# A third attention slot in four steps of the first block: attention one unit further ahead of the MoE loop

## The chip, the core and the metric

One core of a Trainium2 chip runs the whole program. The metric is the device time of one execution in microseconds (us). Of the engines, TensorE (PE; its weight loads are listed as PEld), VectorE (DVE), ScalarE (ACT), GpSimd (POOL) and the queues that issue DMAs (SP, POOL, ACT) appear below.

## What is computed

The reference chains three layers over 2304 tokens (4 batches of 576) with 512 features, in float32:

```python
scores = scale * q @ k.T                      # 8 heads of 64 columns
scores = where(0 <= pos_q - pos_k < 64, scores, -1e9)
attn = exp(scores - max); attn = attn / (sum(attn) + 1e-9)
x = attn @ v                                  # to (2304, 512)
h = x @ w_in                                  # (512, 2048)
g = where(h >= 1, h, where(h <= -1, 0, (h + 1)**2 / 4))
x = g @ w_out                                 # (2048, 512)
h = x @ w_in2                                 # (512, 1024)
solu = h * softmax(h)
out = (layernorm(solu) * g_ln) @ w_out2       # (1024, 512)
```

The window of 64 positions makes attention cheap: a tile of 192 queries needs 256 keys.

## The kernel before

**Tiling.** Tokens are cut into 12 tiles of 192 (`TT`), and two tiles make one of 6 blocks of 384 (`NB`, `NBLK`). Attention works in *units* g = 0 to 47: one tile and one pair of heads, four units to a tile, eight to a block. From unit 18 on (`PU` = 9) two units are done as one *pair*, P = g/2. The first MoE layer runs per block j over 16 slices f of the hidden size.

**One unit** has these stages, and each needs the one before it: S(g) (`st_s`), scores on PE into a PSUM bank, then three masked reductions with a running maximum on DVE (L360), then three exponentials on ACT (L366); norm (`st_norm`), a sum, a reciprocal and a product on DVE (L377, L378, L386); T(g) (`st_t`), three transposes on PE (L402) and a copy on ACT (L407); V(g) (`st_v`), the product with v on PE (L421), then the high part xh of x on ACT (L428) and the low part xl on DVE (L429). `st_qkt` transposes q and k for a later unit on DVE (L317, L326) into one of two buffers `kq0` and `kq1`. For a pair the scores are pS (`pair_s`: L442 on PE, L452 on DVE, L458 on ACT) and the product is pV (`pair_v`, L476).

**One MoE step** (j, f) is H(j,f), 12 matmuls into one bank (`moe_h`, L496: every float32 product is done as high·high + high·low + low·high), the activation on ACT and DVE (L505, L506, L511, L512), the low part of g (L516, on POOL in block 0, on DVE later), and two steps afterwards Y(j,f), 12 matmuls into four accumulators (`moe_y`, L527). After f = 15 the accumulators are copied out (`moe_out`, L537 and L539) and stored. In block 0 the weights of this layer arrive from DRAM as 64-bit numbers and are converted on ACT (L132, L145) and DVE (L136, L137, L146: the lower parts), one unit of weights for `w_in` and one for `w_out` per slice.

**Order.** The code is a list of steps `seq`: block 0 first in two half blocks for f = 0 and 1, then in whole steps f = 2 to 15, then blocks 1 to 5. The generator `slots` cuts the attention into slots, four of them per unit up to unit 16; a step takes `n0` slots before its weight conversion and `n1` after it, one each, and block 0 takes exactly 40, which ends with T(16) and S(17). A scheduler then orders each engine's instructions: it takes the first in the code's order whose inputs and buffers it expects to be ready. Every engine executes its list in that order.

**PSUM.** Block 0 has two banks for attention (`ps_at`), two for H (`ps_h`) and four accumulators. Before H(1,0) both small pools are closed, and a ring of four banks (`ps_ring`) takes their place for all later H and attention. A ring bank becomes free when the last reader of its old tile is done.

Of the kernel before, what the change touches and what calls it, by code (L numbers as in the profile page):

```python
# [20 lines left out]
def kernel(  # L21
# [73 lines left out]
    def at_bank(name):  # L95
        if spare:
            spare.append(spare.pop(0))
            if spare[-1] is not None:
                return ps_acc.tile([128, 512], F32, tag=spare[-1], name=name)
        if ring:  # L100
            return ring[0].tile([128, 512], F32, tag="r", name=name)
        return ps_at.tile([128, 512], F32, tag="a", name=name)
# [47 lines left out]
    def w_conv(start=True):  # L150
        if w_b:
            split_c(*w_b.pop(0))
        if w_a:
            w_b.append(w_a.pop(0))
            split_b(*w_b[-1])
        if w_raw and start:
            w_a.append(w_raw.pop(0))
            split_a(*w_a[-1])
# [72 lines left out]
    def w2_vals(k):  # L231
        for y, a in (("B1", 0), ("B2", 2)):
            z = d_p.tile([128, 2, 512], F32, tag="st", bufs=4, name="w2v")
            for c in range(2):
                nc.sync.dma_start(out=z[:, c, :], in_=w2d[2 * (k + a) + c])
                w2v[f"{y}{c + 1}", k] = z[:, c, :]

    def w2_sums(k):
        for tag, a, b in (("e", "T1", "T2"), ("s", "T3", "T4")):
            z = d_p.tile([128, 2, 512], F32, tag=tag, bufs=3, name="w2t")  # L240
            w2v[a, k], w2v[b, k] = z[:, 0, :], z[:, 1, :]
        for y, a, b in (("T1", "B12", "B11"), ("T2", "B22", "T1"), ("T3", "B22", "B12"), ("T4", "B21", "T2")):
            nc.gpsimd.tensor_tensor(w2v[y, k], w2v[a, k], w2v[b, k], op=ALU.subtract)
# [244 lines left out]
    FIRST, SECOND, WHOLE = slice(0, TT), slice(TT, NB), slice(0, NB)  # L488

    def moe_h(j, f, c):  # L490
        ps = h_bank()[:, c]
        n = 0
        for kc in range(KC):
            hi, lo = wih[f][:, kc, :], wil[f][:, kc, :]
            for a, bb in ((hi, xh[j]), (hi, xl[j]), (lo, xh[j])):
                nc.tensor.matmul(ps, a, bb[:, kc, c], start=(n == 0), stop=(n == 3 * KC - 1))  # L496
                n += 1
        return ps

    def moe_g(part, ps):  # L500
        c = part[2]
        u = wk_p.tile([128, NB], F32, tag="u", name="u")[:, c]
        hi = wk_p.tile([128, NB], F32R, tag="gh", bufs=3, name="gh")[:, c]
        lo = wk_p.tile([128, NB], F32R, tag="gl", bufs=3, name="gl")[:, c]
        nc.scalar.activation(u, ps, ACTF.Relu, bias=half, scale=0.5)  # L505
        nc.scalar.activation(u, u, ACTF.Square)  # L506
        gh[part[0], part[1], part[2].start], gl[part[0], part[1], part[2].start] = hi, lo
        return ps, u, hi, lo

    def moe_g2(ps, u, hi, lo):  # L510
        g = nc.vector.scalar_tensor_tensor(u, u, 1.0, ps, op0=ALU.min, op1=ALU.max)  # L511
        return nc.scalar.copy(hi, u).ins, g.ins  # L512

    def moe_g3(j, ps, u, hi, lo):
        eng = nc.gpsimd if j == 0 else nc.vector
        eng.tensor_tensor(lo, u, as_f32(hi), op=ALU.subtract)  # L516


    def moe_y(j, f, c):
        if f == 0 and c.start == 0:  # L520
            for e in range(KC):
                acc[j, e] = ps_acc.tile([128, 512], F32, tag=f"acc{e}", bufs=1, name=f"acc{e}")
        hi, lo = gh.pop((j, f, c.start)), gl.pop((j, f, c.start))
        for e in range(KC):
            wh, wl = woh[f][:, e * 128:(e + 1) * 128], wol[f][:, e * 128:(e + 1) * 128]
            for n, (a, bb) in enumerate(((wh, hi), (wh, lo), (wl, hi))):
                nc.tensor.matmul(  # L527
                    acc[j, e][:, c], a, bb,
                    start=(f == 0 and n == 0 and c.start == 0), stop=(f == NF - 1 and n == 2),
                )  # L530

    def moe_out(j, es):
        for e in es:
            xo = wk_p.tile([128, NB], F32, tag="u" if j == NBLK - 1 and e > 1 else "xo", name="xo")
            a = acc.pop((j, e))[:, 0:NB]
            if e % 2 == 0:
                nc.scalar.copy(xo, a)  # L537
            else:
                nc.vector.tensor_copy(xo, a)  # L539
            nc.gpsimd.dma_start(out=x2d[j][e], in_=xo)  # L540
# [9 lines left out]
    def w_load(n=1):  # L550
        for _ in range(n):
            if wq:
                w_raw.append(w1_unit(*wq.pop(0)))
# [96 lines left out]
    def slot(n):  # L650
        for _ in range(n):
            next(stages, None)
# [7 lines left out]
    def x2_load(p):  # L660
        r = x2r[p] = d_p.tile([128, KC, 256], F32, tag="x2", bufs=2, name="x2r")
        c = 0
        while c < 256:
            j, c0 = divmod(256 * p + c, NB)
            n = min(256 - c, NB - c0)
            nc.sync.dma_start(out=r[:, :, c:c + n], in_=x2d[j][:, :, c0:c0 + n].rearrange("e p n -> p e n"))
            c += n
# [174 lines left out]

    P_STEPS = {8: "P1", 9: "P6", 10: "P7", 12: "P5", 14: "P4"}

    na = 32 - 4 * G0
    seq = [(0, f, c) for c in (FIRST, SECOND) for f in range(F0)]
    seq += [(j, f, WHOLE) for j in range(NBLK) for f in range(F0 if j == 0 else 0, NF)]
    for n in range(len(seq) + 2):
        if n < len(seq):
            j, f, c = seq[n]  # L850
            last = j == NBLK - 1
            n0 = n1 = 1
            if c == FIRST:
                z = na * (f + 1) // F0 - na * f // F0
                n0, n1 = z - z // 2, z // 2
            if j == 1 and f == 0:
                fr_ctx.close()
                ring.append(ps_ctx.enter_context(
                    tc.tile_pool(name="ps_ring", bufs=4, space=PSUM, reuse_waits="tile")
                ))  # L860
            if last and f == 0:
                at_ctx.close()
                d_p = ctx.enter_context(tc.tile_pool(name="d", bufs=2, side="right", reuse_waits="tile"))
                x2_load(0)
            if j == 1 and f == 4:
                gl_row = wk_p.tile([128, NB], F32, tag="xo", name="gl_row")[0:DF2 // 128, 0:128]
                nc.sync.dma_start(
                    out=gl_row.rearrange("k (b i) -> k b i", b=4),
                    in_=g_ln.rearrange("(b k i) -> k b i", b=4, i=32),
                )  # L870
            if j == 1 and f == 7:
                ps = at_bank("ps_g")
                nc.tensor.transpose(ps[:, 0:DF2 // 128], gl_row, ident[0:DF2 // 128, 0:DF2 // 128])
                nc.vector.tensor_copy(gl_sb, ps[:, 0:DF2 // 128])
            part = moe_g(seq[n], moe_h(j, f, c))
        if n >= 1 and n - 1 < len(seq):
            moe_g3(seq[n - 1][0], *prev)
        if n < len(seq):
            prev = part
            slot(n0)  # L880
            w_conv()
            pins = moe_g2(*part)
        if n >= 2:
            jy, fy, cy = seq[n - 2]
            moe_y(jy, fy, cy)
            if fy == NF - 1:
                moe_out(jy, (0, 1))
        if n < len(seq):
            slot(n1)
            w_conv()  # L890
            if j == 0:
                w_load(2)
            w2_step(n, *pins)
            if last and f < 2:
                w2_vals(f)
            if last and f in (2, 3):
                w2_sums(f - 2)
            if last and f >= 2:
                with tc.issue_after(pins[0]):
                    w2_split(f - 2)  # L900
            if last and 2 <= f < 10:
                w2_load(f - 2)
        else:
            w_conv()
        if n >= 2 and fy == NF - 1:
            moe_out(jy, (2, 3))
        if n < len(seq):
            if last and f == 1:
                x2_load(1)
            if last and f == 5:  # L910
                with tc.issue_after(pins[0]), tc.issue_after(pins[1]):
                    x2_prep(0)
            if last and f in P_STEPS:
                st_p(0, P_STEPS[f])
            if last and f == 14:
                l2_norm(0)
            if last and f == 15:
                st_p(1, "P2")
        elif n == len(seq):
            x2_load(2)  # L920
            x2_prep(1)
            st_p(1, "P3")
            l2_norm(1)
# [63 lines left out]
```

## Time and profile before

| | us |
|---|---|
| median of three runs | 706.68 |
| lowest and highest | 705.14, 708.43 |
| profiled execution | 705.73 |
| its span, first to last instruction | 704.0 |
| PE busy in the span | 681.7 (97%) |
| DVE busy | 442.6 (63%) |
| ACT busy | 411.8 (58%) |

Shares over the whole span mix stages with different limits. The loading of the first layer's weights takes about the first 120 us; the attention is finished by about 432 us; the second MoE layer begins while block 5 of the first still runs. A row of the timeline has the start (us from the start of the span), the duration, the engine, the line, the operation and its tiles, and in brackets the idle time before it with what ended that. Matmuls overlap in the pipeline, so a duration is longer than the distance to the next start.

### The profile page before, as it was taken

How to read it: one execution, taken by the hardware profiler on the slowest of the kernel's cores; microseconds unless marked ns; L12 is line 12 of the kernel's file. 1: busy time of each engine (PE TensorE's matmuls, PEld its weight loads, DVE VectorE, ACT ScalarE, POOL GpSimd, SP SyncE). 2: the span in 40 equal slices, each digit the busy share in tenths (PEclk: the TensorE clock that was granted, in tenths of full speed). 3: DMA queues.
4: the chain of work that ended last, by engine and by line, in shares of the span. 5: the costliest groups of instructions: out<-in, count | busy, mean ns of one | idle time of the engine just before them, and what ended most of it. 6: DMA issues, size and time to landing. Idle time of an engine off the chain costs nothing.

```text
span 704.0 us, 12616 instructions
## 1 busy us (share of the span) xinstructions
PE 681.7 (97%) x4439; PEld 627.7 (89%) x4439; DVE 442.6 (63%) x1179; ACT 411.8 (58%) x1006; POOL 147.6 (21%) x185
## 2 busy tenths in 40 slices
PE   6889999899999999999999999999999999999998
PEld 5689888799999999999999999999987788888887
DVE  4669998556455555454455553642379999988850
ACT  5779777565556655565566565354454746345451
POOL 2313222200001000021112111652272322220000
PEclk9989999999999999999999999999999999999999
DMA  9996798534354524346352211562024465534321
GB/s 188 206 277 179 191 245 215 121 62 108 72 115 106 119 65 77 75 129 125 86 113 67 99 48 43 173 200 92 1 102 123 150 194 166 183 131 141 127 93 46
DMA packets 155543, 88.94 MB, mean 126 GB/s; under 512 B 118616, under 2 KB 141400, under 8 KB 155480
## 3 DMA queue, kind: packets, MB, share of 16 engines
q1 hardware_dynamic: 144040, 64.00, 36.9%
q0 software_dynamic: 8704, 19.41, 8.4%
q10 hardware_dynamic: 2736, 4.72, 1.8%
q8 instruction: 35, 0.57, 0.4%
q14 instruction: 28, 0.23, 0.1%
HBM read 63.97 MB, written 24.12 MB: 125 GB/s over the span
## 4 chain that ended last, share of the span: by engine, by line
PE 74%; DVE 9%; issue 6%; ACT 5%; DMA 4%; POOL 2%; SPq 1%; DVEq 0%; POOLq 0%; ACTq 0%
PE ps_h L496 22%; PE acc L527 22%; PE ps_o L826 13%; PE P L711 8%; DMA wst<-in_moe_w_in_dram 2%; PE ps_x L476 2%; POOL wil L249 2%; PE ps_p L402 2%; PE ps_s L442 2%; PE ps_s L352 1%; ACT p L366 1%; DVE wst L137 1%; DVE gl L516 1%; PE ps_x L421 1%; DVE s L740 1%
## 5 line engine op out<-in xcount | busy, mean ns | idle before, releaser
L511 DVE SCALAR_TENSOR_TENSOR u<-u,ps_h 128x384 f32<-128x384 f32 (+1 forms) x98 | 53.2, 543 | 140.2 <-ACT u L506 139.2
L496 PE MATMUL ps_h<-xh,wih 128*128 128x384 f32 (+1 forms) x392 | 132.1, 338 | 3.1 <-DVE u L511 2.1
L496 PE MATMUL ps_h<-xl,wih 128*128 128x384 f32 (+1 forms) x392 | 131.5, 336 | 0.6 <-DVE xl L429 0.5
L527 PE MATMUL acc<-gl,woh 128*128 128x384 f32 (+1 forms) x392 | 130.5, 334 | 1.5 <-DVE gl L516 1.3
L496 PE MATMUL ps_h<-xh,wil 128*128 128x384 f32 (+1 forms) x392 | 131.4, 335 | 0.0
L527 PE MATMUL acc<-gh,wol 128*128 128x384 f32 (+1 forms) x392 | 129.5, 333 | 0.0
L527 PE MATMUL acc<-gh,woh 128*128 128x384 f32 (+1 forms) x392 | 128.5, 342 | 0.5 <-ACT gh L512 0.5
L505 ACT ACTIVATE u<-ps_h,half 128x384 f32<-128x384 f32 (+1 forms) x98 | 56.0, 572 | 92.7 <-PE ps_h L496 92.5
L512 ACT CAST gh<-u 128x384 fp32r<-128x384 f32 (+1 forms) x98 | 49.7, 507 | 54.6 <-DVE u L511 37.4
L496 PEld LDWEIGHTS ps_h<-xh,wih 128*128 128x128 f32 x392 | 74.3, 190 | 4.9 <-DVE u L511 3.3
L527 PEld LDWEIGHTS acc<-gh,woh 128*128 128x128 f32 x392 | 72.7, 189 | 3.8 <-issue 2.6
L527 PEld LDWEIGHTS acc<-gl,woh 128*128 128x128 f32 x392 | 73.7, 188 | 2.6 <-DVE gl L516 1.7
L516 DVE TENSOR_TENSOR gl<-u,gh 128x384 fp32r<-128x384 f32 x80 | 52.4, 655 | 37.2 <-ACT gh L512 36.7
L496 PEld LDWEIGHTS ps_h<-xl,wih 128*128 128x128 f32 x392 | 74.5, 190 | 1.2 <-DVE xl L429 0.9
L496 PEld LDWEIGHTS ps_h<-xh,wil 128*128 128x128 f32 x392 | 74.6, 190 | 0.1
L527 PEld LDWEIGHTS acc<-gh,wol 128*128 128x128 f32 x392 | 73.6, 188 | 0.1
L711 PE MATMUL P<-wih,x2p 128*128 128x512 f32 x216 | 70.8, 391 | 1.4 <-DVE xo L539 0.9
L826 PE MATMUL ps_o<-woh,wol 128*128 128x512 f32 (+1 forms) x152 | 57.7, 380 | 0.3 <-DVE wol L814 0.3
L826 PE MATMUL ps_o<-woh,woh 128*128 128x512 f32 (+1 forms) x152 | 57.7, 379 | 0.0
L826 PE MATMUL ps_o<-wol,woh 128*128 128x512 f32 (+1 forms) x152 | 57.5, 378 | 0.0
L506 ACT ACTIVATE u<-u 128x384 f32<-128x384 f32 (+1 forms) x98 | 51.1, 522 | 1.9
L711 PEld LDWEIGHTS P<-wih,x2p 128*128 128x128 f32 x216 | 40.4, 188 | 10.4 <-DVE xo L539 1.3
(125 smaller groups left out, 1208.8 us busy)
## 6 DMA issues: line engine op xcount, KB each, us to landing
vw<-in_v_dram SPq DMA_DIRECT2D x32, 256.0 KB, 5.1
wst<-in_moe_w_in_dram SPq DMA_DIRECT2D x16, 512.0 KB, 5.8
wst<-in_moe_w_out_dram SPq DMA_DIRECT2D x16, 512.0 KB, 4.7
lnd<-e SPq DMA_DIRECT2D x16, 512.0 KB, 2.8
lT<-lnd SPq DMA_DIRECT2D x64, 128.0 KB, 2.9
x2d<-xo POOLq DMA_DIRECT2D x24, 192.0 KB, 2.5
out_dram<-o ACTq DMA_DIRECT2D x17, 256.0 KB, 2.0
wst<-in_moe_w_in_dram POOLq DMA_DIRECT2D x8, 512.0 KB, 5.5
```

The costliest lines, as they stand in the source:

```text
L249: nc.gpsimd.tensor_tensor(lo, v_, as_f32(hi), op=ALU.subtract)
L402: nc.tensor.transpose(ps[:, i * 128:i * 128 + 128], p[:, i, :], ident)
L442: nc.tensor.matmul(ps[x][64 * c:64 * c + 64, i * 128 + c0:i * 128 + 128], z[r, KQ + i * 64:KQ + i * 64 + 64], z[r, i * 64 + c0:i * 64 + 12 ...
L496: nc.tensor.matmul(ps, a, bb[:, kc, c], start=(n == 0), stop=(n == 3 * KC - 1))
L505: nc.scalar.activation(u, ps, ACTF.Relu, bias=half, scale=0.5)
L506: nc.scalar.activation(u, u, ACTF.Square)
L511: g = nc.vector.scalar_tensor_tensor(u, u, 1.0, ps, op0=ALU.min, op1=ALU.max)
L512: return nc.scalar.copy(hi, u).ins, g.ins
L516: eng.tensor_tensor(lo, u, as_f32(hi), op=ALU.subtract)
L527: nc.tensor.matmul(acc[j, e][:, c], a, bb, start=(f == 0 and n == 0 and c.start == 0), stop=(f == NF - 1 and n == 2),)
L711: nc.tensor.matmul(ps, l, r, start=(n == 0), stop=(n == 5))
L826: nc.tensor.matmul(ps, a[kk // 4][:, kk % 4, :], b[kk][:, c:c + w], start=(n == 0), stop=(n == 3 * NK2 - 1),)
```

## The change

Four steps of block 0, f = 4, 7, 10 and 13, take two slots after the conversion instead of one:

```diff
+    AHEAD = (4, 7, 10, 13)
     na = 32 - 4 * G0
 ...
             if c == FIRST:
                 z = na * (f + 1) // F0 - na * f // F0
                 n0, n1 = z - z // 2, z // 2
+            if j == 0 and c == WHOLE and f in AHEAD:
+                n1 = 2
             if j == 1 and f == 0:
                 fr_ctx.close()
```

Block 0 so takes 44 slots instead of 40. The four that come over from block 1 are: norm(17) and the transposes for unit 18; V(16), T(17) and the transposes for unit 19; V(17) and the scores pS(9) of the first pair; norm of that pair. No instruction is added or removed. On PE the order up to H(0,10) and Y(0,8) is the same; from there on units 12 to 15 move by up to a step, and every later pair stands two steps earlier than before.

**PE at the end of block 0.** `vw_1293` to `vw_1297` and `vw_1261` to `vw_1265` are the values of the tile with units 16 to 19; `ps_h_1848` and `ps_h_1936` are H(1,0), `ps_h_1924` is H(1,1). Before, from T(16):

```order
L402 MATMUL ps_p_1824<-ident_66,p_1734 128x128 x3
L352 MATMUL ps_s_1830<-kq1_125 128x128 x3
L496 MATMUL ps_h_1848<-xh_767,wih0_146 128x384
...
L421 MATMUL ps_x_1897<-pT_1825,vw_1293 64x64 x2
...
L402 MATMUL ps_p_1906<-ident_66,p_1831 128x128 x3
L496 MATMUL ps_h_1924<-xh_767,wih1_168 128x384
...
L421 MATMUL ps_x_1943<-pT_1907,vw_1293 64x64 x2
...
L442 MATMUL ps_s_1952<-kq0_124 64x128
```

After:

```order
L402 MATMUL ps_p_1758<-ident_66,p_1682 128x128 x3
L352 MATMUL ps_s_1764<-kq1_125 128x128 x3
L421 MATMUL ps_x_1826<-pT_1759,vw_1261 64x64 x2
...
L402 MATMUL ps_p_1835<-ident_66,p_1765 128x128 x3
L421 MATMUL ps_x_1870<-pT_1836,vw_1261 64x64 x2
...
L442 MATMUL ps_s_1879<-kq0_124 64x128
...
L442 MATMUL ps_s_1880<-kq0_124 64x128
...
L496 MATMUL ps_h_1936<-xh_767,wih0_146 128x384
```

V(16), T(17), V(17) and pS(9) stood among the matmuls of H(1,0) and H(1,1); now all of them stand ahead of H(1,0).

**DVE at the same place**, from the end of S(17)'s reductions. `xl_1896` and `xl_1825` are the low parts of V(16) and V(17), `ps_s_1952` and `ps_s_1879` the first half of pS(9). Before:

```order
L377 TENSOR_SCALAR sm_1833<-sm_1833 128x3
L378 RECIPROCAL rs_1867<-sm_1833 128x3
L386 TENSOR_TENSOR p_1831<-p_1831,rs_1867 128x384
L539 COPY xo_2013<-acc3_754 128x384
L429 TENSOR_TENSOR xl_1896<-ps_x_1897,xh_1895 128x192
L511 SCALAR_TENSOR_TENSOR u_1861<-u_1861,ps_h_1848 128x384
L516 TENSOR_TENSOR gl_1863<-u_1861,gh_1862 128x384
L429 TENSOR_TENSOR xl_1896<-ps_x_1943,xh_1895 128x192
```

After:

```order
L429 TENSOR_TENSOR xl_1825<-ps_x_1826,xh_1824 128x192
L377 TENSOR_SCALAR sm_1767<-sm_1767 128x3
L378 RECIPROCAL rs_1796<-sm_1767 128x3
L386 TENSOR_TENSOR p_1765<-p_1765,rs_1796 128x384
L539 COPY xo_2033<-acc3_754 128x384
L429 TENSOR_TENSOR xl_1825<-ps_x_1870,xh_1824 128x192
L452 ISA p_1895,mx_1881<-ps_s_1879,mask_67 128x128
```

Both low parts and the reductions of pS(9) now stand ahead of every activation of block 1. The bank of H(1,0) was that of S(17)'s scores; it is now that of `ps_s_1879`, so H(1,0) waits for the third reduction of L452.

**DVE ahead of H(0,15)**, which waits for the activation of H(0,13) (`u_1675` before, `u_1707` after) to free its bank. Before:

```order
L146 TENSOR_TENSOR wil15_1335<-wst_1336,wih15_1334 128x512
L511 SCALAR_TENSOR_TENSOR u_1675<-u_1675,ps_h_1662 128x384
L429 TENSOR_TENSOR xl_768<-ps_x_1525,xh_767 128x192
L377 TENSOR_SCALAR sm_1496<-sm_1496 128x3
L146 TENSOR_TENSOR wol15_1409<-wst_1410,woh15_1408 128x512
L378 RECIPROCAL rs_1534<-sm_1496 128x3
L382 TENSOR_TENSOR p_1494<-p_1494,rs_1534 128x64
```

After:

```order
L146 TENSOR_TENSOR wil15_1362<-wst_1363,wih15_1361 128x512
L377 TENSOR_SCALAR sm_1453<-sm_1453 128x3
L137 SCALAR_TENSOR_TENSOR wst_1429<-wst_1429 128x512
L378 RECIPROCAL rs_1491<-sm_1453 128x3
L511 SCALAR_TENSOR_TENSOR u_1707<-u_1707,ps_h_1694 128x384
L429 TENSOR_TENSOR xl_768<-ps_x_1482,xh_767 128x192
L382 TENSOR_TENSOR p_1451<-p_1451,rs_1491 128x64
```

Unit 14's sum and reciprocal have moved ahead of the activation; L137 for the last weights, which stood some rows higher before, is the same work in another place.

## Rows read from the trace of the kernel before

**Rows 1.** Windows: busy us (instructions) of PE, PEld, DVE, ACT, POOL; clock; DMA.

```profile
100.00:120.00 20.00, 19.22 (x129) 17.82 (x128) 17.81 (x49) 16.19 (x43) 5.75 (x6) 1.00 0.98 239
160.00:180.00 20.00, 20.00 (x155) 19.20 (x155) 11.14 (x35) 11.37 (x31) 1.09 (x2) 1.00 0.43 94
```

**Rows 2.** Waits of PE from 150 us on: total us, times, longest.

```profile
PE acc L527 <- DVE gl L516: 1.3, 1, 1.3
```

**Rows 3.** Chain that ended last, block 0 to block 1: start, us, what.

```profile
133.44 0.14 issue
133.58 0.52 PE ps_p L402 x3
134.09 0.69 PE ps_s L352 x6
...
135.58 2.35 PE ps_h L496 x12
137.93 0.50 PE ps_x L421 x12
138.43 0.48 PE ps_p L402 x3
...
141.03 0.50 PE ps_x L421 x12
141.52 0.82 PE ps_s L442 x24
142.35 1.94 PE acc L527 x10
144.28 2.08 PE ps_h L496 x12
```

**Rows 4.** Timeline of DVE: norm(17), low part of V(17), reductions of pS(9).

```profile
136.44 0.17 DVE L377 TENSOR_SCALAR sm<-sm 128x3 f32<-128x3 f32 x1 [0.35 <-ACT p L366]
136.64 0.18 DVE L378 RECIPROCAL rs<-sm 128x3 f32<-128x3 f32 x1
136.85 0.56 DVE L386 TENSOR_TENSOR p<-p,rs 128x384 f32<-128x384 f32 x1
...
141.94 0.36 DVE L429 TENSOR_TENSOR xl<-ps_x,xh 128x192 fp32r<-128x192 f32 x1 [0.91 <-ACT xh L428]
...
143.47 0.25 DVE L452 CUSTOM_DVE_ANT_0 p<-ps_s,mask 128x128 f32<-128x128 f32 x1
...
144.08 0.08 DVE L452 DVE_READ_ACCUMULATOR2_ANT mx<- 128x1 f32 x1
```

**Rows 5.** Timeline of ACT: end of S(17)'s exponentials, copy of T(17), V(17)'s high part.

```profile
136.22 0.18 ACT L366 ACTIVATION_READ_ACCUMULATOR p<-p,mx 128x1 f32 x1
...
139.13 0.48 ACT L407 COPY pT<-ps_p 128x384 f32<-128x384 f32 x1
...
141.60 0.31 ACT L428 CAST xh<-ps_x 128x192 fp32r<-128x192 f32 x1
```

**Rows 6.** Windows with the granted clock, columns as in rows 1.

```profile
32.00:34.00 2.00, 0.40 (x12) 0.26 (x10) 1.36 (x5) 2.00 (x7) 0.91 (x1) 1.00 0.40 65
34.00:36.00 2.00, 1.56 (x10) 1.56 (x10) 2.00 (x5) 2.00 (x6) 0.39 (x1) 0.74 0.61 197
38.00:40.00 2.00, 2.00 (x14) 1.88 (x11) 0.11 (x1) 0.58 (x2) 0.00 (x0) 0.50 1.20 305
40.00:42.00 2.00, 2.00 (x19) 1.71 (x18) 1.46 (x9) 1.55 (x8) 0.00 (x0) 0.55 1.34 222
132.00:134.00 2.00, 0.63 (x12) 0.52 (x9) 1.17 (x4) 0.80 (x4) 0.54 (x1) 1.00 0.52 156
```

**Rows 7.** Timeline of PE: three waits in block 0.

```profile
34.44 0.55 PE L402 MATMUL ps_p<-ident,p 128*128 128x128 f32 x3 [2.04 <-POOL p L386]
98.02 0.45 PE L496 MATMUL ps_h<-xh,wih 128*128 128x384 f32 x1 [0.83 <-DVE u L511]
119.70 0.44 PE L496 MATMUL ps_h<-xh,wih 128*128 128x384 f32 x1 [0.76 <-DVE u L511]
```

## Prediction

> **What bounds the kernel now.** I read the windows first, for the limits differ by stage. While the weights of block 0 arrive, nothing is idle: from 100 to 120 us PE is busy 19.2 of 20, DVE 17.8, and the DMA engines 98% of the time [rows 1]. PE does no more than 129 instructions there, and what it waits for is DVE: the waits ahead of H(0,11) and H(0,15), 0.83 and 0.76 us, end with an activation that stands in DVE's list among weight conversions [rows 7]. From block 1 on PE alone sets the pace: 20.00 of 20 us from 160 to 180 [rows 1], and from 150 us to the end it has four waits, of which the longest is 1.3 [rows 2]. So an attention instruction costs its full PE time in blocks 1 to 5, and could cost nothing in a PE wait of block 0. The chain that ended last shows the place between the two [rows 3]: T(16) at 133.58 comes after a norm, then S(17), then H(1,0) at 135.58, which had to wait for S(17)'s reductions to free its bank; from there the chain is PE without a break. V(16), T(17), V(17) and pS(9) stand in it between matmuls of H(1,0) and H(1,1): while PE does those, ACT and DVE prepare the next attention stage, and nobody waits.
>
> **The change, part by part.** No instruction is added, so the sum is made of what moves from under cover or under it.
>
> *The first two extra slots* (f = 4 and 7) move nothing on PE: the order there is the old one, since attention was not held back by slots but by its inputs. Cost 0.
>
> *Block 0 from H(0,11) to S(16).* Units 12 to 15 stand up to a step earlier on PE. DVE has the same work ahead of H(0,15)'s release, and two small instructions more, unit 14's sum and reciprocal; the same two took 0.17 and 0.18 us for unit 17 [rows 4], 0.35 in all. Queued behind them on DVE are the activation, behind that on PE H(0,15), and behind that the end of the block. With DVE at 89% not all of it need count. I take 0.3. The bounds: 0.8 less, if T(12) and S(13), which now stand ahead of H(0,11), fill its wait of 0.83 [rows 7]; 0.9 more, if T(14), now after 2 matmuls of H(0,15) instead of 9, waits for its product. The weights' DMAs and those for q and k change places by a few rows on SP only, and the number of q and k loads ahead of the last weight is the same: 0. On POOL two stores of a later block change places with a load for the second layer, far from any wait: 0.
>
> *The turn to block 1.* This is the large term. I follow the chain with the old durations and the old start of S(17). Its exponentials ended at 136.22 + 0.18 = 136.40; ACT now has V(16)'s high part between them, 0.31 [rows 5], so 136.71. The norm began 0.04 later and took 0.97 (136.44 to 137.41) [rows 4]: 137.72. T(17) follows after 0.14, as T(16) did, and takes 0.48 [rows 3]: 138.34. The copy, 0.48 [rows 5]: 138.82. V(17), 0.05 later and 0.50 long [rows 3]: 139.37. Its high part starts 0.07 later (141.03 + 0.50 to 141.60), its low part 0.34 after that and takes 0.36 [rows 4, 5]: 140.14. Then come three reductions of pS(9), whose matmuls have run meanwhile: 143.47 to 144.16, 0.69 [rows 4], so 140.83. Only then is the bank of H(1,0) free: it starts at 140.9, where it started at 135.58. That is 5.3 later. The wait of H(1,0) is a new one in place of an old, and behind it on PE stands all of block 1. In return the four attention stages are gone from between the matmuls: from H(1,0) to Y(1,0) there were 142.35 - 135.58 = 6.77, and H(1,0) and H(1,1) alone take 2.35 + 2.08 = 4.43 [rows 3], so 2.3 come back. Net 3.0. Bounds 2.3 (the cast does not delay the exponentials, copies overlap more) and 3.7 (V to its high part as slow as with a busy ACT). Nothing of this is gained back: PE is full from here to the end in both kernels, and the later pairs cost the same two steps earlier.
>
> *The clock.* From 133.58 to 140.9 PE now does T(16), S(17), V(16), T(17), V(17) and pS(9): 0.52 + 0.69 + 0.50 + 0.48 + 0.50 + 0.82 = 3.5 us of work in 7.3 [rows 3], and between V(16), which ends near 135.2, and V(17) at 138.87 only T(17). The rows show what such a stretch can do. From 32 to 34 us PE was busy 0.40 of 2.00, with one wait of 2.04; the granted clock then fell from 1.00 to 0.50, the 2.4 and the 1.2 GHz levels, and came back before 42 [rows 6, 7]. The low time is 1.04 us in the window from 34, 2 and 2 in the next two, and 1.8 in the one from 40: 6.8 us. At the old turn, 0.63 busy of 2.00 from 132 to 134, the clock stayed at 1.00 [rows 6]. The new gap is longer than the one that let it fall. If it falls by 136 and is back by 142.8, half of the 1.9 us of dense work that it covers is lost, 0.95; if it falls as H(1,0) begins, half of 6.8, 3.4. I take the middle, 2.2.
>
> The Trainium skill, page "TensorE: Matmul & The Clock Gate", section "HAM oscillation — how this bites in real kernels", speaks of waits in which TensorE does nothing at all between bursts, and those are longer than any single gap here. The trace does not bear that out as a limit, since the fall of rows 6 followed a single wait of 2.04 us; by the page's wording the clock term would be 0 and the sum that of the first rival.
>
> Sum: 0.3 + 3.0 + 2.2 = 5.5. On the profiled execution, 705.73 (a span of 704.0 and 1.73 around it), this gives 711.2. The median of the three runs is 0.95 above that execution, and on it the sum would be 712.2; the runs themselves lie 3.3 apart, so I put the forecast between, at 711.6.
>
> **The rivals.** *The clock holds.* The same chain without the clock term: 705.73 + 3.3 = 709.0. For it speaks that PE has six short pieces of work in the stretch, and that the old turn, with two waits, kept the clock. Against it, the gap around T(17).
>
> *Faster: attention fills PE's waits in block 0.* The mechanism the slots would serve: if H(1,0) started by 135.58 + 2.3 = 137.9 us, the 2.3 us of attention taken out of block 1 would be a gain. At best all of it is, 703.4. It needs S(17) to come 3 us earlier, out of the waits of rows 7 and DVE's slack. Against it: S(16) stands behind the same four matmuls of Y(0,15) as before, and the norms between S(16), T(16) and T(17) are a chain of latencies that no earlier slot shortens.
>
> *Worse: the bounds add up.* 3.7 at the turn, 0.9 in block 0, 3.4 for the clock: 8.0, so 713.7. That the change does nothing is no rival: pS(9) does stand ahead of H(1,0).
>
> **How the numbers follow.** The forecast (turn and clock) has 0.54, the clock holds 0.34, faster 0.06, worse 0.06. A measurement here tells about 0.5% from no change, 3.5 us. The forecast lies above that for nearly all of its bounds (about 0.48 of 0.54), the holding clock mostly below (0.04 of 0.34 above), and worse wholly above: slower 0.58. Faster by more than 0.5% needs more than the whole 2.3 and some wait besides: 0.03. The rest, 0.39, is within 0.5%. The range takes in the clock that holds, with the turn's lower bound (705.73 + 2.3 = 708.0, less a little for block 0), and most of worse: 707.4 to 714.0.
>
> **What would show it.** In the profile of the changed kernel: H(1,0) some 5 us later after S(17) than before, its wait ended by a reduction of L452; T(17) and V(17) each with a wait ahead of them, ended by DVE's L386 and ACT's L407; a window near 136 to 141 with PE far from full; and H(1,0) and H(1,1) without attention between them. A clock column below 1.00 between 136 and 148 decides between forecast and first rival. From 150 us on, the distance of any instruction of block 2 to its old place should stay what it is at H(1,2). I am wrong if H(1,0) starts within 2.3 us of its old place, if block 0 up to S(16) moves by more than 1 us either way, or if the difference grows or shrinks in blocks 1 to 5.

## The result, and the profile of the changed kernel

The changed kernel takes 713.71 us (median of 6 runs, 711.19 to 716.25) and the kernel before 706.10 (6 runs). The ratio is 1.0105, with an interval of 1.0073 to 1.0137: slower, 0.3 us below the upper end of the range. A second measurement, in the experiments below, gave 1.0124 (1.0097 to 1.0152) and a median of 715.34, which is above the range. The profiled execution has a span of 711.49 us where that of before had 703.97, a difference of 7.52 us to be explained.

In the stages from 100 to 120 us and from 160 to 180, PE's load is what it was to within 0.3 us, and DVE has 1.1 us more in the first and 2.2 less in the second [rows 1]:

```profile
100.00:120.00 20.00, 18.91 (x125) 17.49 (x124) 18.88 (x52) 17.02 (x44) 6.01 (x6) 1.00 0.98 245
160.00:180.00 20.00, 20.00 (x155) 19.21 (x154) 8.90 (x24) 10.94 (x28) 1.09 (x2) 1.00 0.35 77
```

The place to look at is the turn to block 1. The windows with PE's busy time first and the granted clock third from the right (columns as in [rows 6]):

```profile
132.00:134.00 2.00, 0.97 (x8) 0.67 (x7) 1.12 (x5) 0.55 (x3) 0.60 (x2) 1.00 0.76 203
134.00:136.00 2.00, 1.30 (x20) 1.04 (x18) 1.16 (x7) 1.31 (x5) 0.00 (x0) 1.00 1.10 298
136.00:138.00 2.00, 0.20 (x2) 0.23 (x3) 1.61 (x6) 1.01 (x5) 0.54 (x1) 1.00 0.76 147
138.00:140.00 2.00, 1.43 (x21) 1.13 (x21) 0.27 (x2) 0.80 (x2) 1.07 (x2) 0.85 0.75 209
140.00:142.00 2.00, 1.96 (x23) 1.59 (x20) 0.93 (x7) 0.64 (x3) 0.00 (x0) 0.50 0.85 226
144.00:146.00 2.00, 2.00 (x8) 2.00 (x7) 1.85 (x6) 0.33 (x2) 0.00 (x0) 0.50 0.25 39
146.00:148.00 2.00, 2.00 (x13) 2.00 (x12) 0.55 (x1) 1.16 (x3) 0.00 (x0) 0.94 0.33 52
```

PE does 0.20 us of work from 136 to 138, and the clock then goes from its 2.4 GHz to its 1.2 GHz level and comes back before 148: 8 matmuls stand in the 2 us from 144, and 13 in those from 146. The chain that ended last (start, us, what) says what PE waited for; it answers to [rows 3]:

```profile
133.61 0.52 PE ps_p L402 x3
134.13 0.68 PE ps_s L352 x6
...
137.80 0.53 PE ps_p L402 x3
138.33 0.02 issue
138.35 0.49 ACT pT L407
138.84 0.04 issue
138.88 0.57 PE ps_x L421 x12
139.45 2.38 PE ps_s L442 x22
141.83 0.01 issue
141.84 8.53 PE ps_h L496 x36
```

H(1,0) starts at 141.84, where it started at 135.58. Ahead of it stand T(17), its copy, V(17) and pS(9), one behind the other. The timeline of PE shows the waits of T(17) and V(17) in brackets:

```profile
137.80 0.52 PE L402 MATMUL ps_p<-ident,p 128*128 128x128 f32 x3 [2.50 <-DVE p L386]
138.88 0.57 PE L421 MATMUL ps_x<-pT,vw 128*64 128x64 f32 x12 [0.57 <-ACT pT L407]
```

### The profile page after: what moved, and what is told of

Its sections match the earlier page's. It is cut to its first block, busy times and chain, and to the rows that moved or that the text cites. A ratio compares the mean times of both kernels' runs of the same rounds, so it can differ in the third digit from the quotient of the medians.

```text
span 711.5 us, 12627 instructions
## 1 busy us (share of the span) xinstructions
PE 688.7 (97%) x4439; PEld 633.8 (89%) x4439; DVE 442.2 (62%) x1179; ACT 412.4 (58%) x1006; POOL 151.4 (21%) x185
## 4 chain that ended last, share of the span: by engine, by line
PE 78%; DVE 7%; issue 6%; ACT 4%; DMA 3%; POOL 2%; SPq 1%; DVEq 0%; POOLq 0%; ACTq 0%
PE ps_h L496 24%; PE acc L527 23%; PE ps_o L826 13%; PE P L711 8%; PE ps_x L476 2%; PE ps_s L352 2%; PE ps_p L402 2%; PE ps_s L442 2%; POOL wil L249 2%; DMA wst<-in_moe_w_out_dram 1%; ACT p L366 1%; PE ps_x L421 1%; DMA wst<-in_moe_w_in_dram 1%; DVE gl L516 1%; DVE wst L137 1%
```

## Where the 7.52 us lie

Three starts on the timeline of PE cut the difference into parts: T(16), H(1,2) and H(4,14). From H(4,14) on both kernels run in the same order. At H(1,2) ten matmuls of Y(1,0) are done in the kernel before [rows 3] and none in the changed one, so 1.74 us is added to the changed one's place (24 matmuls of a step without attention take 4.16 us). "Turn" is the change of the distance from T(16) to H(1,2), "later" that of the distance from H(1,2) to H(4,14). The other kernels are those of the experiments. Up to T(16) all but "two slots" have the changed kernel's order on PE, and T(16) lies between 1.71 us earlier and 1.81 later in them: so far do executions of that order differ.

| kernel | T(16) | H(1,2) | H(4,14) | turn | later | low clock at the turn |
|---|---|---|---|---|---|---|
| before | 133.58 | 144.12 | 431.13 | | | none |
| changed | 133.61 | 148.13 | 438.65 | 5.72 | 1.77 | 6.8 us |
| changed, again | 132.95 | 148.58 | 439.11 | 6.83 | 1.78 | 10.2 us |
| V(P) in one piece | 135.39 | 150.08 | 438.82 | 5.89 | 0.0 | 6.8 us |
| the same, again | 135.21 | 150.81 | 439.54 | 6.80 | 0.0 | 10.2 us |
| fill | 131.87 | 143.84 | 434.38 | 3.17 | 1.79 | none |
| fill, V(P) in one piece | 133.46 | 145.44 | 434.18 | 3.18 | 0.0 | none |
| two slots | 135.70 | 147.48 | 436.25 | 2.98 | 0.0 | none |
| pay back | 132.58 | 143.14 | 430.15 | 0.0 | 0.0 | none |

In the profiled pair T(16) is 0.03 later, the turn costs 5.72 and what follows 1.77. The last of these has no term in the prediction. It comes in four steps of 0.42 to 0.46 us, one in each of the blocks 1 to 4, at the first pV of the block. There the scheduler put three matmuls of Y between the first matmul of pV and the other eleven. The timeline shows it in block 4 (a row of L476 counts both halves of the array):

```profile
387.85 0.34 PE L527 MATMUL acc<-gh,woh 128*128 128x384 f32 x1
388.11 0.33 PE L476 MATMUL ps_x<-pT,vw 128*64 128x64 f32 x2
388.37 0.45 PE L527 MATMUL acc<-gh,woh 128*128 128x384 f32 x1
388.66 0.34 PE L527 MATMUL acc<-gl,woh 128*128 128x384 f32 x1
388.83 0.34 PE L527 MATMUL acc<-gh,wol 128*128 128x384 f32 x1
389.10 0.91 PE L476 MATMUL ps_x<-pT,vw 128*64 128x64 f32 x22
```

Two matmuls of the MLP start 0.17 apart; here it is 0.26 from one to pV's first, 0.26 from that to the next of the MLP, 0.29 from there to its second, and 0.27 from its third back to pV. In the order of the kernel before no pV is split.

## Experiments

**Pay back.** Is it the slots in block 0, or what they do at the turn?

```diff
+            if j == 0 and c == WHOLE and f >= 14:
+                n0 = n1 = 0
```

> The four third slots of block 0 stay; the steps f = 14 and 15 of block 0 get no slots, so that four are taken back and the order of PE from H(1,0) to the end is that of the kernel before, with no V(P) split. Theory (the loss lies at the turn to block 1, in the clock there and in four split V(P), and nowhere else): 706.1 us plus or minus 1, ratio 1.000 to the kernel before; H(1,0) at 135.3 to 136.0 us, granted clock 1.00 from 130 to 150 us, H(5,14) within 0.6 us of its place before. Rival (the slots in block 0 cost the time, by DVE work that is put ahead of the weights' conversions, or by the loads that move with them): 710 to 713 us, with the difference already there at S(16).

707.32 us against 706.70, ratio 1.0003 (0.9986 to 1.0021). The granted clock stays at 1.00 through the turn, H(1,0) starts at 134.59, and every start behind it is 0.98 earlier than in the kernel before, as T(16) is 1.00 earlier. So the third slots by themselves cost nothing that the times can tell, and the rival, with 710 to 713, falls.

**Fill.** Thirteen matmuls that nobody uses stand in PE's new wait, in the banks of T(17) and V(17) ahead of their own work.

```diff
+        if u == GB + 1:
+            for _ in range(10):
+                nc.tensor.matmul(ps[:, 0:NB], wih[15][:, 0, :], xh[1][:, 0, :], start=True, stop=True)
 ...
+        if g == GB + 1:
+            for _ in range(3):
+                nc.tensor.matmul(ps[:, 0:NB], wih[15][:, 0, :], xh[1][:, 0, :], start=True, stop=True)
```

> The changed kernel with 13 extra 128x384 matmuls on PE (10 written into the bank of T(17), 3 into that of V(17), all overwritten), which stand between V(16) and T(17), where PE waits 2.50 us; the order is otherwise that of the changed kernel. Theory (the fall of the clock is caused by the thin stretch of PE and costs 3.1 us by itself): granted clock 1.00 from 130 to 150 us, H(1,0) at 140.6 to 141.0 us instead of 141.84, H(1,2) at 145.0 instead of 148.13, and 710.6 us in all, 3.1 below the changed kernel. Rival (the clock falls for another reason, or the wait of H(1,0) is the whole loss): the clock still falls, 713.7 us or more.

710.68 us, ratio 1.0063 (1.0040 to 1.0085): the time is the forecast to 0.1. The trace is not quite: H(1,0) came at 139.58 and H(1,2) at 143.84, in an execution that was 1.71 earlier at T(16), and counted from there H(1,2) is 2.55 earlier than in the changed kernel where 3.1 was forecast. The windows:

```profile
134.00:136.00 2.00, 2.00 (x12) 2.00 (x13) 1.61 (x6) 1.27 (x6) 0.44 (x1) 1.00 0.91 181
136.00:138.00 2.00, 1.43 (x22) 1.09 (x22) 0.37 (x1) 0.57 (x2) 1.17 (x3) 1.00 0.67 177
138.00:140.00 2.00, 1.96 (x26) 1.50 (x23) 1.51 (x8) 1.12 (x6) 0.00 (x0) 1.00 0.81 179
```

More work on PE made the changed kernel some 3 us faster. The fall is caused by PE's thin stretch, and the turn costs 3.17 us without it. The timed runs agree: the mean granted clock has a median of 0.990 in the nine runs with the filling, as in the kernel before, and of 0.986 in the twelve of the changed kernel. Of these the filling itself costs 0.18: T(17) starts 4.37 us after T(16) with it (133.46 to 137.83 in the kernel with both repairs) and 4.19 without (133.61 to 137.80). So the wait of H(1,0) for attention is worth 3.0 us and the low clock 2.7 to 2.9 where it lasts 6.8 us, 3.8 where it lasts 10.2.

**V(P) in one piece.** With the halves in the other order, pV's first matmul needs the copy that ends last, so nothing goes between.

```diff
-                for x in range(2):
+                for x in (1, 0):
```

> The changed kernel with the two halves of each V(P) in the other order (x = 1 before x = 0), whereby its first matmul needs the copy that ends last, and no matmul of the second layer of the MLP stands between its first and its second any more; the order up to H(1,3) is that of the changed kernel. Theory (four split V(P), in blocks 1 to 4, cost 0.42 to 0.46 us each beyond the turn): 711.9 us, 1.8 below the changed kernel, and the distance from the kernel before stays the same from H(1,6) to H(5,14), while it grew by 1.3 to 1.8 there in the changed kernel. Rival (the growth comes from the earlier places of the pairs, not from the split): 713.7 us, with the same growth.

713.70 us, ratio 1.0095 (1.0070 to 1.0120): the time shows no gain and is the rival's. The trace does: from H(1,2) on nothing is lost (column "later", 0.0). But this execution was 1.81 us later at T(16) than the kernel before, and so came out at the same span. Whether that belongs to the edit was left open, and both were run again, on one chip.

> The changed kernel once more, beside the next run, since the profiled execution of the first run with V(P) in one piece was 1.8 us later than the changed kernel's already ahead of T(16). Both theories: 713.7 us, ratio 1.0105 to the kernel before; the distance from the kernel before grows by 1.8 us between H(1,2) and H(5,14).

> V(P) in one piece once more, on the chip and beside the runs of the changed kernel. Theory (a split V(P) costs 0.44 us, four of them 1.8): 711.9 us, 1.8 below the changed kernel of this call; the distance from the kernel before stays the same from H(1,2) on. Rival (the gain in blocks 1 to 4 is real in the trace and comes back as time ahead of T(16), where the order of the halves can do nothing, or is eaten by a longer time at the lower clock): 713.7 us, and again later than the changed kernel ahead of T(16).

The changed kernel took 715.34 us, ratio 1.0124 (1.0097 to 1.0152), and V(P) in one piece 713.19, ratio 1.0085 (1.0057 to 1.0113), 2.2 less. "Later" was again 1.78 and 0.0. pV now stands in one row:

```profile
389.89 0.34 PE L527 MATMUL acc<-gh,wol 128*128 128x384 f32 x1
390.16 0.92 PE L476 MATMUL ps_x<-pT,vw 128*64 128x64 f32 x24
```

By the times alone the two intervals still overlap. The traces of six kernels settle it: with the split 1.77 to 1.79, without it nothing. T(16) was again 1.6 us late in the second profile with one piece, and 0.6 early in the changed kernel's, whose block 0 has the same order. That the edit has no part in this is likely, since the kernel with both repairs has T(16) 0.12 early, but not shown.

**Both repairs.**

> Both repairs at once: 13 extra matmuls on PE between V(16) and T(17), all overwritten, and V(P) in one piece. Theory (clock and split V(P) are two separate terms, and what is left is the wait of H(1,0) for attention): 706.7 plus 2.6 = 709.3 us, ratio 1.0037 to the kernel before; in the trace the distance from the kernel before, counted from T(16), is 2.3 to 2.7 us at H(1,2) with the ten matmuls of Y(1,0) counted in, and the same at H(5,14). Rival (V(P) in one piece gains nothing): 710.7 us, ratio 1.0063.

708.97 us, ratio 1.0039 (1.0019 to 1.0059). The two terms add. What is left in the trace is the turn's own 3.2 us, where 2.3 to 2.7 were expected; the times put it at 2.8, between 1.3 and 4.2.

**Two slots.** Half of the change: `AHEAD = (10, 13)`.

> Half of the change: third slots in f = 10 and 13 alone, so that V(16) and T(17), but not V(17) and pS(9), stand ahead of H(1,0), and no V(P) is split. Theory (the terms add: the wait of T(17) stays, 2.5 us long, H(1,0) follows it; and such a wait lets the clock fall): H(1,0) at 138.3 to 138.8 us, 2.7 to 3.2 later, less 0.98 for V(16) and T(17), which is 1.8 to 2.2 at H(1,2); 2.7 for the clock; nothing after: 711.2 us, ratio 1.0065 to the kernel before. Rival (it is the pair's scores and their reductions that cost, not T(17)): 707 us, H(1,0) within 1 us of its old place.

710.97 us, ratio 1.0066 (1.0039 to 1.0093), on the forecast, but for a different reason than I gave. In the profiled execution the clock held:

```profile
138.00:140.00 2.00, 0.11 (x1) 0.14 (x2) 1.61 (x6) 0.74 (x4) 0.00 (x0) 1.00 1.26 268
```

with the wait of T(17) in the middle of it, and H(1,0) behind it waiting for T(17)'s copy to free its bank:

```profile
139.89 0.30 PE L402 MATMUL ps_p<-ident,p 128*128 128x128 f32 x1 [2.41 <-DVE p L386]
140.97 0.44 PE L496 MATMUL ps_h<-xh,wih 128*128 128x384 f32 x1 [0.57 <-ACT pT L407]
145.29 0.44 PE L496 MATMUL ps_h<-xh,wih 128*128 128x384 f32 x1 [0.63 <-DVE u L511]
```

The turn cost 2.98, where I had put 1.8 to 2.2: the wait for the bank is there, and H(1,1) waits 0.63 more. Whether the clock fell in some of the timed executions stays open. So T(17) ahead of H(1,0) costs as much as T(17), V(17) and pS(9) together do at full clock.

**Two fewer.** The opposite of the change: no slots in the last step of block 0, and none added.

```diff
-    AHEAD = (4, 7, 10, 13)
+    AHEAD = (15,)
 ...
             if j == 0 and c == WHOLE and f in AHEAD:
-                n1 = 2
+                n0 = n1 = 0
```

> The opposite of the change: no third slots, and no slots in the last step of block 0, so that attention runs half a unit less ahead; T(16), S(17), V(16) and T(17) stand behind matmuls of H(1,0), H(1,1) and Y(1,0). Theory (at the turn PE waits for attention that it needn't do yet: 1.37 us ahead of T(16) and 0.81 ahead of H(1,0) in the kernel before): both waits go, 703.9 us, ratio 0.997; clock 1.00 throughout the turn. Rival (the waits come back as others: H(1,0) waits for the low part of V(15), or a later pair comes late in block 1 or ahead of block 2): 706 us or more, ratio 1.000.

706.08 us, ratio 0.9987 (0.9965 to 1.0009), no difference. The wait of H(1,0) had come back as another one, as the rival said, for the bank that V(15) held:

```profile
134.29 0.44 PE L496 MATMUL ps_h<-xh,wih 128*128 128x384 f32 x1 [0.81 <-DVE xl L429]
```

and 0.53 us was lost ahead of the second layer (1.87 instead of 1.34 [rows 2]). Next, the pool of H's banks was opened ahead of that of attention, which makes the ring's first bank one of H's:

```diff
-    ps_at = fr_ctx.enter_context(tc.tile_pool(name="ps_at", bufs=2, space=PSUM))
     ps_h = fr_ctx.enter_context(tc.tile_pool(name="ps_h", bufs=2, space=PSUM))
+    ps_at = fr_ctx.enter_context(tc.tile_pool(name="ps_at", bufs=2, space=PSUM))
```

> No third slots, no slots in the last step of block 0, and the banks of H allocated ahead of those of attention, so that the ring's first bank, which H(1,0) takes, is one of H's and not the one that V(15) holds. Theory (what was left of the wait at the turn with two slots fewer, 0.81 us until the low part of V(15) had been taken, was the wait for that bank): H(1,0) starts right after V(15), no wait above 0.3 us from 128 to 150 us, 705.3 us, ratio 0.9975 to the kernel before. Rival (the inputs of the last head pair, not the bank, hold H(1,0): the wait moves to its tenth or eleventh matmul): 706.1 us, ratio 0.9987.

706.28 us, ratio 0.9996 (0.9977 to 1.0015). In the trace the wait is gone and H(1,2) to H(5,14) are earlier, the last by 1.55 us, of which the timed runs show nothing that can be told from no change. Then the two slots were given back in the first two steps of block 1 (`n1 = 2` for j = 1, f = 0 and 1), so that the order from block 2 on is the old one:

> As the last run with two slots fewer and the other bank, but the two slots are given back in the first two steps of block 1, so that the order from block 2 to the end is that of the kernel before. Theory (the 0.53 us that was lost ahead of the second layer came from another order there; the turn gives 2.4 us): PE's longest wait from 128 to 150 us below 0.3, H(5,14) 2.0 to 2.5 us earlier than in the kernel before, counted from T(16)'s norm; 704.4 us, ratio 0.9967. Rival (what the turn gives is lost again to other places, as the timed runs of that kernel said): 706.5 us, ratio 0.9995.

705.18 us against 707.44, ratio 0.9965 (0.9945 to 0.9985; one run of twelve took 2325 us and is left out). This interval overlaps that of the kernel before it (0.9977 to 1.0015), so it isn't shown that the order from block 2 on is what made the gain. PE has no wait at the turn:

```profile
132.00:134.00 2.00, 2.00 (x20) 1.62 (x20) 1.67 (x8) 1.90 (x8) 0.89 (x2) 1.00 0.01 2
```

**Early fill.** The fall of the clock at 34 us [rows 6, 7] in the kernel before: ten unused matmuls between V(4) and T(6) (`FILL` is `{6: 10}`, and `v_last[0]` the last matmul of V(4)).

```diff
+        if u in FILL:
+            with tc.issue_after(v_last[0]):
+                for _ in range(FILL[u]):
+                    nc.tensor.matmul(ps[:, 0:NB], wih[0][:, 0, :], wih[0].rearrange("p k n -> p (k n)")[:, 0:NB], start=True, stop=True)
```

> The kernel before with 10 extra 128x384 matmuls on PE, written into the bank of T(6) and overwritten, between V(4) and T(6), where PE waits 2.04 us at 32 to 34 us and the clock falls to 0.50 for 6.8 us; the order is otherwise the old one. Theory (that fall too comes from PE's wait, and part of it reaches the end, since over the 49 runs of the kernel before the time rises by 0.3 us for each us at the lower clock): no fall near 35 us, 704.7 us (706.7 less 0.3 times 6.8), ratio 0.997. Rival (block 0 is bounded by VectorE and the weights' loads, which swallow the loss by 100 us): clock 1.00 but 706.7 us, ratio 1.000.

704.39 us, ratio 0.9964 (0.9945 to 0.9982). The clock is 1.00 from 32 us on:

```profile
34.00:36.00 2.00, 2.00 (x18) 1.97 (x18) 2.00 (x5) 2.00 (x7) 0.19 (x1) 1.00 0.88 261
```

**The last two together.**

> The two before this one together: 10 extra matmuls ahead of T(6), and the turn with two slots fewer and the other bank. Theory (the terms add): 702.4 us, ratio 0.994 to the kernel before, clock 1.00 from 24 to 700 us. Rival (neither reaches the end): 706.5 us, ratio 1.000.

700.96 us (700.40 to 701.68) against 707.44, ratio 0.9921 (0.9900 to 0.9942): faster than both kernels of this case, and 1.4 less than the sum that was forecast. The profiled execution's span is 698.6:

```profile
core 0: 698.6 us, clock 1.000
```

## Why the prediction came out as it did

**The chain at the turn** held up to V(17)'s low part. T(17), V(17) and the low part of V(17) were forecast from the old durations with ends at 138.34, 139.37 and 140.14; they ended at 138.33, 139.45 and 140.21. What stands behind them did not. H(1,0) was forecast for 140.9 and came at 141.84, and the clock made only part of that. In the kernel with both repairs, where the clock holds and T(17) starts at 137.83, H(1,0) starts at 141.17. The prediction let the matmuls of pS(9) run while V(17)'s high and low parts were made, 0.82 us of work; its first half did so. But the two banks of `ps_at` are taken in turn, so its second half takes the bank of V(17), and it started at 140.27, right behind the low part that ended at 140.21. The two halves, side by side in the ring of four banks before, went one after the other and took 1.75. The chain and DVE's row in that kernel:

```profile
139.46 0.80 PE ps_s L448 x12
140.26 0.01 issue
140.27 0.92 PE ps_s L448 x12
```

```profile
139.85 0.36 DVE L435 TENSOR_TENSOR xl<-ps_x,xh 128x192 fp32r<-128x192 f32 x1 [1.88 <-ACT xh L434]
```

In the changed kernel the low clock came on top: pS(9) took 2.42 there and ended at 141.80, and the third reduction, forecast for 140.83, ended at 141.68. So the last thing ahead of H(1,0) was pS(9) itself, and not the reduction that was named as a sign:

```profile
139.38 2.42 PE L442 MATMUL ps_s<-kq 64*64 64x128 f32 x24
```

```profile
139.85 0.36 DVE L429 TENSOR_TENSOR xl<-ps_x,xh 128x192 fp32r<-128x192 f32 x1 [1.73 <-ACT xh L428]
...
141.40 0.28 DVE L452 CUSTOM_DVE_ANT_0 p<-ps_s,mask 128x128 f32<-128x128 f32 x1
```

The net price of 3.0 us is all the same what the runs without a fall of the clock show, 3.17 less 0.18 for the filling. This agreement is in part luck, as two misses of 0.2 cancel: with both repairs, counted from T(16) and without the filling's 0.18, H(1,0) is 5.5 later where 5.3 was forecast, and 2.5 us came back behind it where 2.3 was.

**The clock** fell, in all four profiled executions of this order without filling. The term was 2.2, with bounds of 0.95 and 3.4; it was 2.7 to 2.9 in two executions and 3.8 in the other two. The bound was too low because it took the length of the low time from one execution, and 10.2 us occurs as well. The first rival, the clock that holds, is the kernel with both repairs: 709.0 was forecast for it, and 708.97 measured. That they agree so closely is luck: the forecast stands 3.3 above the kernel before, the measured ratio 2.8, with an interval of 1.3 to 4.2.

**Block 0** was put at 0.3 and was 0.03 in the profile; the kernel with the slots paid back is 0.2 above the kernel before in the times, between 1.0 below and 1.5 above, so whether it is 0.3 or nothing stays open. The two waits of H in [rows 7] did go, and others took their place: 0.96 ahead of a transpose that waits for DVE at 98 us, 1.08 ahead of a Y that waits for POOL at 103.

**The step that failed** with a price that no term of the sum holds is one half sentence: "the later pairs cost the same two steps earlier". They don't, as four of them were torn by the scheduler, 1.77 us in all. The order of the changed kernel was there to read before any run; I had compared which stages stand between which steps and not whether a stage is in one piece. With it the sum would have been 7.3 instead of 5.5, and the forecast 713.4; the range held the time because its upper end had been made by other bounds. That the measured 713.71 is also the 713.7 of the rival "worse" is chance: of that rival's bounds, 3.7 at the turn and 0.9 in block 0 were not reached. One of the signs of being wrong that were named beforehand did come, and caught the missing term: the difference grew in blocks 1 to 5.

**The faster rival**, attention in waits of block 0, had no place in the profile: S(16) starts at 129.48 where it started at 129.32, so nothing behind it began earlier. Of the three kernels with fewer slots one shows the opposite direction to be the useful one: 2.4 us from H(0,15) to H(5,14) in the trace (H(5,14) is 0.91 earlier and H(0,15) 1.53 later, in the kernel with the order kept). The other two show no difference in the times.

## What to carry to other kernels

A stage whose inputs come through a chain of short steps on other engines belongs behind independent matmuls, not ahead of them: putting it earlier in an engine's list doesn't make it ready earlier, and everything behind it waits. Follow the banks through such a chain too: a stage counted as hidden may wait for the bank of the one ahead of it, as the second half of pS(9) did. Where one engine is full, read its whole new order for pieces that were cut in two, since here each split cost 0.42 to 0.46 us. And a wait of PE can cost more than its length, where the clock falls with it; there, unused matmuls in the wait can be a gain, as they were in two places here.

## What the runs showed of the hardware

When the low clock begins and how long it lasts change between executions of one program: in the changed kernel, with the same two waits of 2.50 and 0.57, it came at 139.4 us and lasted 6.8 in one profile, and came at 136.9, before the first of the two waits was over, and lasted 10.2 in the other. In the kernel with two slots it did not come, with waits of 2.41 and 0.57. The Trainium skill, page "TensorE: Matmul & The Clock Gate", section "What's actually happening", says of a kernel's start that the count of slow matmuls differs from run to run; these traces show the same for a fall in the middle of a kernel.

A good part of the spread of this kernel's times goes with the granted clock. Over 49 runs of the kernel before, the time rises by 0.3 us for each us at the low level, as worked out from each run's mean granted clock (correlation 0.67). That mean has a median of 0.990; with ten matmuls in one wait of 2 us it was 1.000 in nine runs of twelve. So in those nine a second fall, which the profile of the changed kernel has from 50.7 to 54.1 us, at a wait of 1.17, did not come either. The rival was that block 0 swallows such losses; with the filling 1.2 us were gained to the end in the profile, and 2.5 by the ratio of the times.
